# Three more second-layer groups by seven products, in a new static order, with four late stores issued by ScalarE

## The chip, the core and the metric

The kernel runs on one core of one Trainium2 chip. The metric is the device time of one execution in microseconds (us). TensorE is called PE below, VectorE DVE, ScalarE ACT, GpSimd POOL, and SyncE SP; SP issues nearly all DMAs.

## The reference

An attention with random features is followed by a two-layer network with a residual. All is float32; the batch is 8, there are 8 heads, 576 positions per sequence, head width 64, 128 features, model width 512 and hidden width 2048.

```python
def phi(x):
    proj = np.einsum('bhsd,md->bhsm', x, omega)
    h = proj - np.sum(x * x, axis=-1, keepdims=True) / 2.0
    h = h - np.max(h, axis=-1, keepdims=True)
    return np.exp(h) / np.sqrt(m)
q_p, k_p = (phi(q * scale), phi(k * scale))
kv = np.einsum('bhsm,bhsd->bhmd', k_p, v)
num = np.einsum('bhsm,bhmd->bhsd', q_p, kv)
den = np.einsum('bhsm,bhm->bhs', q_p, np.sum(k_p, axis=2))[..., None] + 1e-06
...
x = (num / den).transpose(0, 2, 1, 3).reshape(B, S, H * D)
xn = (x - mu) / np.sqrt(var + 1e-06) * g_ln
out = x + np.maximum(xn @ w_ch1, 0.0) @ w_ch2
```

## The kernel before

The 4608 rows of x are cut into 36 chunks of 128 rows, and four chunks make a tile of 512. Tiles 0 to 2 go through the two layers in the plain way (`mm1`, `mm2`): for each of 16 slabs of 128 hidden columns, a first-layer product, a relu on ACT and DVE, and a second-layer product that adds into four banks. Tiles 3 to 8 go in three pairs (pair 0, 1 and 2, `gen_pair`). A number is kept as two parts, a high and a low one, and a product is three matmuls: high by high, high by low, low by high.

The first layer of a pair takes two slabs of hidden columns at a time (`one_set`), as a 2 by 2 block product that is done with seven products instead of eight (`product`, 6 matmuls of 512 columns each); the sums of inputs and weights that it needs are made beforehand on DVE (`gen_forms` for the inputs, called A11, S1, S2 and so on; `gen_wform` for the weights), and the partial results are combined in the PSUM banks by copies on ACT and additions on DVE (`gen_copy`, `gen_snap`, `gen_x2`, `gen_y2`).

The second layer of a pair is done in four groups of four slabs, after each two sets. In pairs 0 and 1 a group is plain: eight calls of `one_chunk`, each 12 matmuls of 512 columns for one chunk of 128 rows, 96 in all. In pair 2 a group is two calls of `two_chunks`, each seven products of 12 matmuls of 256 columns (`product2`), 168 in all. The hidden values then need sums and high and low parts of their own (`form_a11` to `form_s4`, `finish`), and so do the second-layer weights (`gen_w2form`).

The attention is woven in between: a block of keys (`gen_k`), the sums over keys (`gen_sums`), the queries' features (`gen_q`) and x itself (`gen_x`) are short visits to PE between the large matmuls, each with work on ACT, DVE and, for the queries' maximum, on POOL. A visit of `gen_k`, `gen_sums` or `gen_x` has matmuls of 64 rows or 64 columns.

Nothing is scheduled on the chip: `Plan` runs on the host, keeps a clock for each engine by fixed costs, and writes the instructions of each engine in one order. The dictionary `SLOT` says at which place of PE's stream each visit is to stand (32 units to a tile, so 160 is the start of pair 1), `SHIFT` moves ranks of parts, and `EARLIER`, `WF`, `MARGIN` and others set costs and due times. Each engine then runs its instructions strictly in the order written, and a wait holds up all that stands behind it on that engine.

```python
        wide = p == NPAIR - 1
...
            if p == NPAIR - 1:
                for h in range(2):
                    yield from two_chunks(gr, h)
                continue
```

Of the kernel before, what the change touches and what calls it, by code (L numbers as in the profile page):

```python
# [75 lines left out]
class Plan:  # L76
# [25 lines left out]
    def __init__(self):  # L102
# [12 lines left out]
        self.pair, self.loan, self.at, self.where = (), (), 0, 0  # L115
# [83 lines left out]
    def go_to(self, at, step):  # L199

        self.at, self.step, self.turn = at, step, 0

    def serve(self, lend):
# [11 lines left out]
        sets = (self.pair,) + (lend and len(due) > 1) * (self.loan,)  # L215
# [10 lines left out]
        if lend and len(cols) == len(todo) > 2 and guests:  # L226
# [74 lines left out]
    def run(self):  # L301
        while self.ready or self.stuck():
# [24 lines left out]
            if eng == SP:  # L327
# [6 lines left out]
                part.end = self.dma_at + (FLOWN if part.want[-1] == "flip" else 0.0)  # L334
# [12 lines left out]
def favor_ffn(ctx, tc, kT, kTr, vF, vR, qT, qD, omT, gT, w1, w2, out):  # L347
# [86 lines left out]
    def slots(pair):  # L434
        i = 512 * int(pair[0][1:])
        return all_banks.rearrange("p a b -> p (a b)")[:, i : i + H * SLOT].rearrange("p (a b) -> p a b", b=SLOT)[:, :, 0 : D + 1]

# [9 lines left out]
    n_hid, n_xnT, n_mb, n_st = names("hid", 2), names("xnT", 1), names("mb", 3), (*names("st", 3), "st3")  # L447
# [3 lines left out]
    turn = {k: names(f"turn_{k}", n) for k, n in (("k", 2), ("q", 2), ("blk", 3), ("mx", 2), ("xn", 3), ("w", 3), ("wl", 5))}  # L451
# [10 lines left out]
    plan.pair, plan.loan = b_at, b_h  # L462
# [413 lines left out]
    def gen_x(c, b_turn):  # L876
# [13 lines left out]
        t_x = yield "get", n_x  # L890
# [105 lines left out]
    def gen_flip(t, i, xn, t_n, xn_turn):  # L996
# [7 lines left out]
        if t >= NREG + 2:  # L1004
            p, u = divmod(t - NREG, 2)
            yield wait("stage", p)
            cols = slice(u * T + i * P, u * T + (i + 1) * P)
            words = stages[p][1].bitcast(U16).rearrange("p k (c b) -> p b k c", b=2)
            eng = yield either(1.27, 1.13)
            copy(eng, words[:, :, :, cols], flipped)  # L1010
            free(t_n, xn_turn, t_p)
            done(("xT", t, i))
            return
# [4 lines left out]
        if t >= NREG:  # L1018
            u = t - NREG
            yield dma(P * DM, -0.4)  # L1020
            nc.sync.dma_start(
                xT_away[:, :, u * T + i * P : u * T + (i + 1) * P], f32(whole).rearrange("p (a b) c -> p a (b c)", b=P)
            )
            free(t_p)
            done(("xT", t, i))
            return
# [125 lines left out]
    def store(c, t_x, x, p, last):  # L1152
        yield dma(P * (p.stop - p.start), -1.1)
        nc.sync.dma_start(out[c * P : (c + 1) * P, p], x[:, p])
        if last:
            free(t_x)

    n_form = ("A11", "S3", "S2", "A12", "S1", "A22", "S4")
# [6 lines left out]
    xT_away = dram.tile([P, NK, 2 * T], F32, tag="xT_away", name="xT_away", bufs=1)  # L1165
# [4 lines left out]
    hforms, fs, w2q, users, halves_left = {}, {}, {}, {}, {}  # L1170
# [61 lines left out]
    def gen_more():  # L1232
# [8 lines left out]
        extra[n_st[-1]] = more[:, 1, 0:48]  # L1241
        free(n_x[N_X + 2], n_st[-1])

    def gen_stage(p):

        if p:
            yield wait("used", 1, NF - 1)
            yield wait("formed", p - 1)
            t_s = yield "get", n_xnT
            st = tile_of(t_s, [P, NK, 2 * T])  # L1250
            stages[p] = [t_s], st
            done(("stage", p))
# [10 lines left out]
        for k in range(NK):  # L1263
            plan.add(plan.cur.rank, gen_stage_k(p, k))

    def gen_stage_k(p, k):
        yield dma(P * 2 * T)
        nc.sync.dma_start(stages[p][1][k], xT_away[:, k])
# [9 lines left out]
    def gen_forms(p):  # L1278
        if p:
            for u in range(2):  # L1280
                for i in range(TC):
                    yield wait("xT", NREG + 2 * p + u, i)
        else:
            for k in range(NK):
                yield wait("xk", p, k)
# [3 lines left out]
        def cut(ap):  # L1289
            return [ap] if n_part == 1 else [ap[:, k] for k in range(2)]  # L1290
# [7 lines left out]
        def split(name, src):  # L1298
            tags, hi, lo = yield from room(name)
            for o, a in zip(cut(hi), src):  # L1300
                yield us(ACT, 0.22 + 0.00083 * 2 * T / n_part)
                nc.scalar.copy(out=o, in_=a)
            for o, a, b in zip(cut(lo), src, cut(f32(hi))):
                yield dve2(2 * T / n_part)
# [4 lines left out]
        def summed(out_, a, b, op):  # L1309
            for o, x, y in zip(out_, a, b):  # L1310
                yield dve2(2 * T / n_part)
                nc.vector.tensor_tensor(out=o, in0=x, in1=y, op=op)

        yield from split("A11", a11)
        t_s = yield "get", n_quad
        s1 = cut(tile_of(t_s, [P, 2, T]))
        yield from summed(s1, a21, a22, ALU.add)
        yield from summed(a21, a11, a21, ALU.subtract)
        yield from split("S3", a21)
        yield from summed(a11, s1, a11, ALU.subtract)  # L1320
        yield from split("S2", a11)
        yield from split("A12", a12)
        yield from split("S1", s1)
        free(t_s)
        yield from split("A22", a22)
        yield from summed(a12, a12, a11, ALU.subtract)
        yield from split("S4", a12)
        free(*stages[p][0])
        done(("formed", p))

# [26 lines left out]
    def gen_ring2(p):  # L1357
        if p:
            yield wait("w2all", p - 1)
        for f in range(NF):  # L1360
# [4 lines left out]
    def gen_w2(p, f, t_w):  # L1365
# [6 lines left out]
        users[p, f] = 2 if p == NPAIR - 2 else 1  # L1372
        done(("w2s", p, f))

    def leave(p, f):
        users[p, f] -= 1
        if not users[p, f]:
            free(w2s[p, f][0])

    def gen_w2form(j):  # L1380
        f, g = 2 * j, 2 * j + 1
        for n in (f, g):
            yield wait("w2s", NPAIR - 2, n)
# [572 lines left out]
```

## Time and profile before

| | before |
|---|---|
| median of 3 runs | 930.6 us (930.43 to 930.69) |
| profiled execution, its own time | 930.92 us |
| span of its instructions | 929.2 us |
| PE busy | 921.2 us, 99% of the span |
| DVE busy | 673.6 us, 72% |
| ACT busy | 503.1 us, 54% |
| POOL busy | 121.1 us, 13% |
| DMA queue of SP | 201.34 MB, 65.6% of 16 DMA engines' time |
| granted clock of PE | 1.00 (2.4 GHz) |

The span runs from the first to the last instruction; the time of an execution is 1.7 us more. PE's busy time joins the modelled spans of its matmuls, which overlap, so how closely it is packed is better read from the starts of matmuls that follow each other. Idle time of the other engines costs nothing unless PE waits for them.

### The profile page before, as it was taken

Reading aid. Unit: us, or ns where it says so; the run is one execution under the profiler, and the core shown is the slowest. Engines: PE = TensorE matmul, PEld = TensorE weight load, DVE = VectorE, ACT = ScalarE, POOL = GpSimd, SP = SyncE. Lnnn points to the kernel's source line nnn. Section 1 sums busy time; section 2 is a strip of 40 time slices with the busy share of each in tenths; the row PEclk is TensorE's granted clock in tenths of the full one; section 3 lists DMA queues with packets and bytes.
Section 4 is the critical chain, followed back from the end, with each engine's and each line's share of the span. In section 5 each row is a group of like instructions: output and inputs, shape, how many; then the busy total and the mean of one; then the engine's idle time right before and its main releaser. Section 6 shows DMA issues by size and latency. Waiting matters only on the chain.

```text
span 929.2 us, 17577 instructions
## 1 busy us (share of the span) xinstructions
PE 921.2 (99%) x6871; PEld 766.9 (83%) x6871; DVE 673.6 (72%) x1178; ACT 503.1 (54%) x915; POOL 121.1 (13%) x47
## 2 busy tenths in 40 slices
PE   9999999999999999999999999999999999999998
PEld 6878777888888888888888888888888888988988
DVE  6999988674758877667566547898836596585765
ACT  7878876565753472437756444557412245253452
POOL 5001314130420041001302110304000000000000
PEclk9999999999999999999999999999999999999999
DMA  8676369996446559295956634796946558574562
GB/s 310 218 269 238 142 180 365 371 347 167 126 115 233 183 152 341 94 369 118 288 176 202 187 110 174 240 385 150 314 149 225 204 203 298 166 285 141 177 226 91
DMA packets 142577, 202.71 MB, mean 218 GB/s; under 512 B 44064, under 2 KB 79008, under 8 KB 142496
## 3 DMA queue, kind: packets, MB, share of 16 engines
q1 hardware_dynamic: 142352, 201.34, 65.6%
q8 instruction: 54, 0.88, 0.4%
q10 hardware_dynamic: 144, 0.26, 0.1%
q14 instruction: 27, 0.22, 0.1%
HBM read 140.74 MB, written 52.43 MB: 208 GB/s over the span
## 4 chain that ended last, share of the span: by engine, by line
PE 92%; DVE 6%; issue 1%; DMA 0%; SPq 0%; ACT 0%; DVEq 0%
PE b L1423 8%; PE b L1425 8%; PE b L1424 8%; PE b L1745 6%; PE b L1746 6%; PE b L1747 6%; PE b L1122 5%; PE b L1078 4%; PE b L1124 4%; PE b L1123 4%; PE b L1080 4%; PE b L1079 4%; PE b L674 4%; PE b L718 3%; PE b L899 3%; PE b L1665 3%
## 5 line engine op out<-in xcount | busy, mean ns | idle before, releaser
L845 POOL PARTITION_ALL_REDUCE quad<-quad x35 | 118.2, 3398 | 517.3 <-ACT quad L392 380.8
L1423 PE MATMUL b<-w,w 128*128 128x512 f32 x336 | 131.9, 392 | 0.0
L1425 PE MATMUL b<-w,w 128*128 128x512 f32 x336 | 130.8, 389 | 0.0
L1424 PE MATMUL b<-w,w 128*128 128x512 f32 x336 | 130.8, 389 | 0.0
L1745 PE MATMUL b<-w,w 128*128 128x512 f32 x256 | 101.2, 395 | 0.0
L1746 PE MATMUL b<-w,w 128*128 128x512 f32 x256 | 99.8, 390 | 0.0
L1747 PE MATMUL b<-w,w 128*128 128x512 f32 x256 | 99.7, 389 | 0.0
L683 ACT ACTIVATE kp<-b,mb 128x128 f32<-128x128 f32 x264 | 72.3, 389 | 26.8 <-DVE mb L677 25.9
L1122 PE MATMUL b<-w,hid 128*128 128x512 f32 x192 | 78.1, 407 | 0.0
L1078 PE MATMUL b<-xnT,w 128*128 128x512 f32 (+1 forms) x200 | 78.1, 390 | 0.0
L1080 PE MATMUL b<-xnT,w 128*128 128x512 f32 (+1 forms) x200 | 76.2, 381 | 0.0
L1079 PE MATMUL b<-xnT,w 128*128 128x512 f32 (+1 forms) x200 | 76.2, 381 | 0.0
L1124 PE MATMUL b<-w,hid 128*128 128x512 f32 x192 | 75.2, 392 | 0.8 <-DVE hid L1096 0.8
L1123 PE MATMUL b<-w,hid 128*128 128x512 f32 x192 | 75.0, 390 | 0.0
L1423 PEld LDWEIGHTS b<-w,w 128*128 128x128 f32 x336 | 63.1, 188 | 14.2 <-ACT b L1481 0.9
L1487 ACT COPY hid<-b 128x512 f32<-128x512 f32 x64 | 37.6, 587 | 68.1 <-PE b L1425 38.7
L1425 PEld LDWEIGHTS b<-w,w 128*128 128x128 f32 x336 | 63.1, 188 | 13.3
L1424 PEld LDWEIGHTS b<-w,w 128*128 128x128 f32 x336 | 63.1, 188 | 12.7
L1481 ACT COPY b<-b 128x512 f32<-128x512 f32 x32 | 18.6, 580 | 83.6 <-PE b L1425 67.8
L1494 DVE TENSOR_TENSOR b<-b,hid 128x512 f32<-128x512 f32 x32 | 22.3, 697 | 56.5 <-ACT hid L1487 56.3
L1096 DVE SCALAR_TENSOR_TENSOR hid<-b,hid 128x512 fp32r<-128x512 f32 x48 | 33.0, 688 | 37.9 <-ACT hid L1094 37.5
L1745 PEld LDWEIGHTS b<-w,w 128*128 128x128 f32 x256 | 48.0, 188 | 10.8
(220 smaller groups left out, 2050.8 us busy)
## 6 DMA issues: line engine op xcount, KB each, us to landing
w<-wf SPq DMA_DIRECT2D x168, 256.0 KB, 5.0
w<-w SPq DMA_DIRECT2D x32, 512.0 KB, 6.6
w<-w2a SPq DMA_DIRECT2D x32, 512.0 KB, 5.7
quad<-qD SPq DMA_DIRECT2D x28, 512.0 KB, 5.1
away<-x SPq DMA_DIRECT2D x33, 256.0 KB, 2.8
w2a<-w SPq DMA_DIRECT2D x16, 512.0 KB, 6.2
wf<-wide SPq DMA_DIRECT2D x32, 256.0 KB, 2.8
w2t<-wide SPq DMA_DIRECT2D x32, 256.0 KB, 3.1
```

The costliest lines, as they stand in the source:

```text
L845: nc.gpsimd.partition_all_reduce(mx.rearrange("p a b -> p (a b)"), qc.rearrange("p a b -> p (a b)"), P, bass_isa.ReduceOp.max)
L1078: nc.tensor.matmul(ph[:, ts], w[:, 0, cs], xnT[:, 0, k, ts], start=k + i0 == 0, stop=False)
L1079: nc.tensor.matmul(ph[:, ts], w[:, 1, cs], xnT[:, 0, k, ts], start=False, stop=False)
L1080: nc.tensor.matmul(ph[:, ts], w[:, 0, cs], xnT[:, 1, k, ts], start=False, stop=k == NK - 1 and i1 == TC)
L1122: nc.tensor.matmul(accs[i][:, c], hl[:, 0, cs], w[:, 0, c], start=(f == 0), stop=False)
L1124: nc.tensor.matmul(accs[i][:, c], hl[:, 1, cs], w[:, 0, c], start=False, stop=f == NF - 1 and c == parts[-1])
L1423: nc.tensor.matmul(o, w[:, 0, cs], hi[:, k], start=first and k == 0, stop=False, skip_group_check=True)
L1424: nc.tensor.matmul(o, w[:, 1, cs], hi[:, k], start=False, stop=False, skip_group_check=True)
L1425: nc.tensor.matmul(o, w[:, 0, cs], lo[:, k], start=False, stop=k == 1, skip_group_check=True)
L1745: nc.tensor.matmul(acc[:, o], hl[:, 0, cs], w[:, 0, o], start=n == 0 and o is parts[0], stop=False)
L1746: nc.tensor.matmul(acc[:, o], hl[:, 0, cs], w[:, 1, o], start=False, stop=False)
L1747: nc.tensor.matmul(acc[:, o], hl[:, 1, cs], w[:, 0, o], start=False, stop=n == 3 and o is parts[-1])
```

## The change

One constant, `G1 = 1`, says that in pair 1 only the first group stays plain; groups 1, 2 and 3 take the two calls of `two_chunks` that pair 2 had. So 288 matmuls of 512 columns go and 504 of 256 columns come. What goes with it:

- The hidden forms are made for these groups too: on DVE and ACT `form_a11` and the like run 14 times each instead of 8.
- The weights' forms (`gen_w2form`) are made before pair 1's second group instead of during pairs 1 and 2, from high and low parts that are loaded for it (32 loads of 256 KB more).
- The inputs of pairs 1 and 2 go through DRAM as pair 0's did (16 stores of 256 KB and 8 loads of 512 KB more) instead of being written into place. Their room lends eight more buffers for x.
- All attention visits must be over before pair 1's second group: the last `gen_x` has slot 168 instead of 179.
- `Plan` may serve visits in a third pair of banks, so that more of them can follow each other directly.
- In the last group of pairs 1 and 2, two of the stores are issued from ACT's queue.
- `SLOT`, `SHIFT`, `EARLIER` and the cost constants are all new, so nearly every engine's order differs.

```diff
+G1 = 1
+ORDERED = 7
+STAGE, FORM_AT, FORM_LAST = ((2, 3, 4, 5), (4, 5, 6, 6)), 7, 22
+W2GO = 19
-W2F = -30
+W2F = (240, 25)
-MARGIN = {ACT: 0.2, DVE: 0.15}
-FLOWN, EDGE = 1.2, (0.1, 0.1)
+MARGIN = {ACT: 0.2, DVE: 0.1}
+FLOWN, EDGE = 1.2, (1.1, 0.1)
-WF = (35, 15.0)
+WF = (46, 19.0)
...
+    def strassen2(p, gr):
+
+        return p == NPAIR - 1 or (p == NPAIR - 2 and gr >= G1)
...
-            if p == NPAIR - 1:
+            if strassen2(p, gr):
                 for h in range(2):
-                    yield from two_chunks(gr, h)
+                    yield from two_chunks(p, gr, h)
                 continue
...
-        sets = (self.pair,) + (lend and len(due) > 1) * (self.loan,)
+        sets = (self.pair,) + self.where * (self.third,) + (lend and (len(due) > 1 or self.where > 0)) * (self.loan,)
...
+        for i in range(2):
+            plan.add(plan.cur.rank, gen_w2in(2 * j + i, r[i], low[i]))
...
+    def gen_w2in(f, r, low):
+        yield dma(2 * P * DM, 0.5)
+        nc.sync.dma_start(r, w2_away[f][:, 0])
+        nc.sync.dma_start(low, w2_away[f][:, 1])
+        done(("w2in", f))
...
-    def store(c, t_x, x, p, last):
-        yield dma(P * (p.stop - p.start), -1.1)
-        nc.sync.dma_start(out[c * P : (c + 1) * P, p], x[:, p])
+    def store(c, t_x, x, p, last, by_act=False):
+        if by_act:
+            yield us(ACT, 0.45)
+        else:
+            yield dma(P * (p.stop - p.start), -1.1)
+        (nc.scalar if by_act else nc.sync).dma_start(out[c * P : (c + 1) * P, p], x[:, p])
...
-                plan.add(MOST_URGENT, store(c, t_x, x, cols, not halves_left[c]))
+                plan.add(MOST_URGENT, store(c, t_x, x, cols, not halves_left[c], h == half == i == 1))
```

**First place: PE, the end of the second set of pair 1's group 1 and what follows.** Before (`b` is a PSUM bank; the lines 1745 to 1747 are `one_chunk`'s three matmuls):

```order
L1423 MATMUL b_74<-w1_100_6139,w2_10_3495 128x512
L1424 MATMUL b_74<-w1_100_6139,w2_10_3495 128x512
L1425 MATMUL b_74<-w2_90_6140,w2_10_3495 128x512
L1745 MATMUL b_74<-w2_100_6727,w1_130_6813 128x512
L1746 MATMUL b_74<-w2_100_6727,w1_130_6813 128x512
L1747 MATMUL b_74<-w2_100_6727,w1_130_6813 128x512
```

Of the change, at the same place (lines 1719 to 1721 are `product2`'s):

```order
L1463 MATMUL b_74<-w1_100_6513,w2_10_3489 128x512
L1464 MATMUL b_74<-w1_100_6513,w2_10_3489 128x512
L1465 MATMUL b_74<-w2_90_6514,w2_10_3489 128x512
L1719 MATMUL b_74<-w2_100_7014,kp0_7079 128x256
L1720 MATMUL b_74<-w2_100_7014,kp0_7079 128x256
L1721 MATMUL b_74<-w2_100_7014,kp0_7079 128x256
```

The 96 rows of 512 columns that stood here have become 168 of 256.

**Second place: DVE in tile 0, where the first-layer weights of slab 9 get their low half** (line 604 is `gen_w`'s last subtraction, 1096 and 1089 the relu's low half, 580, 566 and 588 steps of other weights). Before, as DVE's rows 135 to 139:

```order
L566 SCALAR_TENSOR_TENSOR w2_90_1062<-w2_90_1062,wide4_1136 128x512
L394 CAST w1_90_1176<-wide6_1081 128x512
L400 TENSOR_SCALAR w2_90_1062<-w2_90_1062 128x512
L1096 SCALAR_TENSOR_TENSOR hid1_1159<-b_74,hid1_1159 128x512
L604 TENSOR_TENSOR w1_90_1176<-wide6_1081,w1_90_1176 128x512
```

Of the change, DVE's rows 150 to 155:

```order
L588 TENSOR_TENSOR wide2_1210<-wide2_1210,g_sb_83 128x512
L1089 SCALAR_TENSOR_TENSOR hid0_1277<-b_74,hid0_1277 128x512
L580 SCALAR_TENSOR_TENSOR wide1_1265<-w1_110_1157 128x512
L566 SCALAR_TENSOR_TENSOR w1_130_1165<-w1_130_1165,wide4_1281 128x512
L949 BN_AGGR st0_440<-st0_440 128x2
L604 TENSOR_TENSOR w1_90_1302<-wide2_1210,w1_90_1302 128x512
```

PE's first matmul of that slab stands at nearly the same place in both (row 385 before, 386 of the change), and DVE comes to its weights 16 instructions later, behind the relu of slab 8 instead of beside that of slab 7. Up to DVE's row 60 (the relu of slab 0) and PE's row 214 the two orders of these engines are the same, buffer numbers and one low half of weights (DVE's row 59) aside.

**Third place: the last stores.** Before, SP's last rows:

```order
L1154 DMA out<-x5_7845 128x256
L1154 DMA out<-x2_7885 128x256 x2
L1154 DMA out<-w2_140_4349 128x256 x2
L1154 DMA out<-w2_150_4372 128x256
L1154 DMA out<-x5_7845 128x256
```

Of the change, SP's last rows are the first four here, and ACT's last two rows (after its last copy, line 1534) are the fifth and sixth:

```order
L1150 DMA out<-w2_150_4353 128x256
L1150 DMA out<-x0_8413 128x256 x2
L1150 DMA out<-x2_8429 128x256
L1150 DMA out<-w2_140_4327 128x256
L1150 DMA out<-x2_8429 128x256
L1150 DMA out<-w2_150_4353 128x256
```

The store of the last result, `w2_150`, now stands on a queue that has issued one other store since its last copy.

## Rows read from the trace of the kernel before

**Rows 1.** The page, busy time, share of the span and instructions of each engine

```profile
PE 921.2 (99%) x6871; PEld 766.9 (83%) x6871; DVE 673.6 (72%) x1178; ACT 503.1 (54%) x915; POOL 121.1 (13%) x47
```

**Rows 2.** Timeline, pair 1, group 1: start, length, engine, line; first and next after

```profile
664.16 0.39 PE L1745 MATMUL b<-w,w 128*128 128x512 f32 x1
...
685.92 0.39 PE L1423 MATMUL b<-w,w 128*128 128x512 f32 x1
```

**Rows 3.** Timeline, PE's waits for DVE: idle before and releaser in brackets

```profile
39.48 0.50 PE L1124 MATMUL b<-w,hid 128*128 128x512 f32 x1 [0.29 <-DVE hid L1096]
...
128.15 0.49 PE L1124 MATMUL b<-w,hid 128*128 128x512 f32 x1 [0.54 <-DVE hid L1096]
...
151.84 0.50 PE L833 MATMUL b<-quad,om_hi 128*128 128x512 f32 x1 [0.46 <-DVE kv L746]
...
484.95 0.47 PE L833 MATMUL b<-quad,om_hi 128*128 128x512 f32 x1 [0.16 <-DVE x L910]
```

**Rows 4.** Timeline, pair 2, groups 0 and 2: first matmul, next after

```profile
786.68 0.28 PE L1665 MATMUL b<-w,kp 128*128 128x256 f32 x1
...
806.99 0.40 PE L1423 MATMUL b<-w,w 128*128 128x512 f32 x1
...
826.18 0.28 PE L1665 MATMUL b<-w,w 128*128 128x256 f32 x1
...
846.22 0.40 PE L1423 MATMUL b<-w,w 128*128 128x512 f32 x1
```

**Rows 5.** Timeline, PE around one visit alone and around two together

```profile
304.08 0.39 PE L1124 MATMUL b<-w,hid 128*128 128x512 f32 x1
304.40 2.09 PE L899 MATMUL b<-kv,quad 128*64 128x65 f32 x64
...
306.75 0.40 PE L1123 MATMUL b<-w,hid 128*128 128x512 f32 x1
...
337.09 0.39 PE L1124 MATMUL b<-w,hid 128*128 128x512 f32 x1
337.41 1.15 PE L899 MATMUL b<-kv,quad 128*64 128x65 f32 x32
...
338.83 0.40 PE L1123 MATMUL b<-w,hid 128*128 128x512 f32 x1
```

**Rows 6.** Timeline, the last operations

```profile
924.57 0.87 DVE L1719 SCALAR_TENSOR_TENSOR w<-b,st,w 128x256 f32<-128x256 f32 x2
924.79 1.41 SPq L1154 DMA_DIRECT2D out<-w  x3
925.36 0.48 DVE L1719 SCALAR_TENSOR_TENSOR x<-b,st,x 128x256 f32<-128x256 f32 x1
926.29 0.41 SPq L1154 DMA_DIRECT2D out<-x  x1
```

**Rows 7.** Windows in tile 0 and pair 2: stretch, length, busy time of each engine, clock, DMA

```profile
39.50:99.50 60.00, 60.00 (x422) 47.11 (x424) 59.97 (x109) 49.73 (x108) 5.37 (x2) 1.00 0.70 252
...
768.00:925.00 157.00, 156.83 (x1007) 142.58 (x1005) 105.89 (x192) 68.36 (x120) 0.00 (x0) 1.00 0.59 199
```

**Rows 8.** The chain in order of time, 108 to 111 us: start, length, what

```profile
109.71 0.60 DVE w L604
110.31 1.14 DVE quad L850
```

**Rows 9.** Timeline, POOL's reductions and DVE beside them

```profile
97.37 8.98 POOL L845 PARTITION_ALL_REDUCE quad<-quad  x2 [22.77 <-ACT quad L392]
...
102.58 2.98 DVE L580 SCALAR_TENSOR_TENSOR wide<-w 128x512 uint32<-128x512 uint32 x2
...
124.71 2.13 DVE L394 CAST w<-wide 128x512 fp32r<-128x512 f32 x1
```

**Rows 10.** Windows with full DMA engines, pair 1 and tile 1; columns as in rows 7

```profile
605.00:627.00 22.00, 22.00 (x152) 17.99 (x151) 21.15 (x49) 12.62 (x19) 0.00 (x0) 1.00 1.07 389
...
139.40:232.00 92.60, 92.14 (x853) 74.21 (x852) 64.29 (x116) 57.17 (x109) 20.30 (x6) 1.00 0.97 313
```

More of the change, by code (lines that the diff above doesn't have):

```diff
@@ L114, in __init__ @@
         self.mlp = None
-        self.pair, self.loan, self.at, self.where = (), (), 0, 0
+        self.pair, self.loan, self.third, self.at, self.where, self.zone = (), (), (), 0, 0, 0
         self.shared = {}
@@ L197, in lodge, with go_to @@
         self.shared.update(dict.fromkeys(four, 0.0))
-    def go_to(self, at, step):
-        self.at, self.step, self.turn = at, step, 0
+    def go_to(self, at, zone, where, step):
+        self.at, self.zone, self.where, self.step, self.turn = at, zone, where, step, 0
     def serve(self, lend):
@@ L225, in serve @@
         guests = [p for p in cols if p.want[3]]
-        if lend and len(cols) == len(todo) > 2 and guests:
+        if lend and not self.where and len(cols) == len(todo) > 2 and guests:
             todo.remove(guests[0])
@@ L333, in run @@
                 self.landed.append(self.dma_at)
-                part.end = self.dma_at + (FLOWN if part.want[-1] == "flip" else 0.0)
+                part.end = self.dma_at + (FLOWN if part.want[-1] == "flip" else 0.0) + LAND * late
             else:
@@ L889, in gen_x @@
         total = st[:, 44 + i : 45 + i]
-        t_x = yield "get", n_x
+        if t >= ORDERED:
+            yield wait("place", c - 1)
+        t_x = yield "get", n_x + n_room
+        done(("place", c))
         t_d = yield "get", n_dn
@@ L1359, in gen_ring2 @@
             yield wait("w2all", p - 1)
-        for f in range(NF):
+        for f in range(NF if p < NPAIR - 2 else 4 * G1):
             t_w = yield "get", n_ring2
@@ L1544, in form_a11, with form_a22 @@
         free(b_a)
-        done(("f", j, "A11"))
-        yield from finish(j, "A11")
-    def form_a22(j, s):
-        a22 = yield from whole(j, "A22")
+        done(("f", p, j, "A11"))
+        yield from finish(p, j, "A11")
+    def form_a22(p, j, s):
+        a22 = yield from whole(p, j, "A22")
         eng = yield either(0.5, 0.34)
@@ L1555, in form_a22, with form_a21 @@
         free(s)
-        done(("f", j, "A22"))
-        yield from finish(j, "A22")
-    def form_a21(j, b_c):
+        done(("f", p, j, "A22"))
+        yield from finish(p, j, "A22")
+    def form_a21(p, j, b_c):
         rank = plan.cur.rank
-        a21 = yield from whole(j, "A21")
+        a21 = yield from whole(p, j, "A21")
         yield act(T)
@@ L1599, in form_a12, with form_s4 @@
             free(b_b)
-    def form_s4(j, b_b, left_b):
-        yield wait("f", j, "S2")
-        yield wait("a12", j)
-        s4 = yield from whole(j, "S4")
+    def form_s4(p, j, b_b, left_b):
+        yield wait("f", p, j, "S2")
+        yield wait("a12", p, j)
+        s4 = yield from whole(p, j, "S4")
         yield dve(T)
         nc.vector.scalar_tensor_tensor(
-            out=s4, in0=bank(b_b), scalar=0.0, in1=fs[j, "S2"][1], op0=ALU.max, op1=ALU.subtract
+            out=s4, in0=bank(b_b), scalar=0.0, in1=fs[p, j, "S2"][1], op0=ALU.max, op1=ALU.subtract
         )
@@ L1659, in product2 @@
             w = w2q[t_w]
-            for i in range(2):
-                o = bank(t_b)[:, i * HALF : (i + 1) * HALF]
-                cs = slice((2 * h + i) * P, (2 * h + i + 1) * P)
-                yield us(PE, 0.36)
-                fresh, last = first and i == s == 0, s == 1
-                nc.tensor.matmul(o, hl[:, 0, cs], w[:, 0], start=fresh, stop=False, skip_group_check=True)
-                nc.tensor.matmul(o, hl[:, 0, cs], w[:, 1], start=False, stop=False, skip_group_check=True)
-                nc.tensor.matmul(o, hl[:, 1, cs], w[:, 0], start=False, stop=last, skip_group_check=True)
@@ L1668, in product2 @@
-            if h:
-                free(tag, t_w)
-    def two_chunks(gr, h):
-        ta, j = NREG + 2 * (NPAIR - 1), NF + 2 * gr + h
-        b_a, b_d, b_b, b_c = (banks[0], banks[1], banks[6], banks[7]) if h == 0 else (banks[2], banks[3], banks[5], banks[4])
-        sk, p = snaps[h], NPAIR - 1
+            o = bank(t_b)[:, i * HALF : (i + 1) * HALF]
+            cs = slice((2 * h + i) * P, (2 * h + i + 1) * P)
+            yield us(PE, 0.36)
+            fresh, last = first and i == s == 0, s == 1
@@ new lines, in product2, with two_chunks @@
+            nc.tensor.matmul(o, hl[:, 0, cs], w[:, 0], start=fresh, stop=False, skip_group_check=True)
+            nc.tensor.matmul(o, hl[:, 0, cs], w[:, 1], start=False, stop=False, skip_group_check=True)
+            nc.tensor.matmul(o, hl[:, 1, cs], w[:, 0], start=False, stop=last, skip_group_check=True)
+            if h and i:
+                free(tag, t_w)
+    def two_chunks(p, gr, h):
+        ta, j = NREG + 2 * p, NF + 2 * gr + h
+        b_a, b_d = b_acc[2:4] if h else b_at
+        b_b, b_c = turned()
+        sk = snaps[h]
```

318 lines of the change are left out of this document (176 added, 142 removed).

## The prediction

> **What bounds the kernel now.** I read the page's busy shares first: PE is busy 99% of the span, and no other engine over 73% [rows 1]. Since a matmul's span is modelled and overlaps the next one, I then read the starts of matmuls in a plain group of pair 1: its 96 matmuls of 512 columns take from 664.16 to 685.92 us, 21.76 us [rows 2], or 0.227 us each without a gap. From 39.5 us to the end the whole stream looks like that, but for the short attention visits and four places where PE waits for DVE [rows 3]. An idle time there begins at the modelled end of a matmul, about 0.16 us after the place where the next start would have been; with that added the four waits are 0.46, 0.70, 0.62 and 0.32 us, together 2.1 us. So the time is PE's work, plus the first 39 us, in which the two orders agree, plus these waits, plus the tail after the last matmul. Anything that takes matmuls away shortens the kernel, unless DVE, ACT or the DMA queue comes too late for the shorter stream.
>
> **What the change costs, part by part.**
>
> The matmuls. Three groups of 96 matmuls of 512 columns go. What comes in their place exists in pair 2: 168 matmuls of 256 columns take 20.04 us in its group 2 (826.18 to 846.22) and 20.31 us in its group 0 (786.68 to 806.99, with a small wait in it) [rows 4]. A group so gains 1.45 to 1.72 us, three gain 4.4 to 5.2; I take 4.9. The gain is small because a narrow matmul costs 20.04 / 168 = 0.119 us, more than half of 0.227. The Trainium skill, "TensorE: Matmul & The Clock Gate", section "Back-to-back issue gap", gives a gap of columns / 2.4 GHz and some 2.5 ns at full clock. By that the gain would be 288 x 0.2158 - 504 x 0.1092 = 7.1 us. The trace does not agree with the page, both sizes run about 11 ns longer here, and the trace decides.
>
> The visits. Their number and kinds stay, but more of them follow each other directly. A visit alone costs, from the start of the last large matmul to the start of the second one behind it, 338.83 - 337.09 = 1.74 us, less two steps of 0.227: 1.29 us. Two together cost 306.75 - 304.08 - 0.45 = 2.22 us [rows 5]. So a visit is 0.93 us of work and a turn of PE between large and small matmuls 0.36 us. Counting in the two orders the places where PE turns to visits with 64 rows or columns after the first large matmul, I find 64 before and 59 now: 5 x 0.36 = 1.8 us less. Bounds: 0, if the pieces that now meet in new mixes pay a change of kind of their own, and 2.2.
>
> The tail. The last DVE operation ends at 925.36 + 0.48 = 925.84 us, but its store is issued at 926.29, because SP's queue is busy with three earlier stores until 926.20 [rows 6]. On ACT's queue, idle by then, it can start at about 925.95: 0.35 us less; bounds 0 and 0.45.
>
> Tile 0. From 39.5 to 99.5 us DVE is busy 59.97 of 60.00 us [rows 7]: here weights are split, and DVE is as much the bound as PE. A step of 512 elements costs DVE 0.60 us when it runs back to back, one of 1024 elements 1.14 [rows 8]. Both orders agree up to the relu of slab 0, which ends at 39.4 us. In the new order the low half of slab 9's first-layer weights comes 95 DVE instructions later: 79 of 0.60, 5 of 1.14 and 11 short ones, 54.2 us, so at 93.6 us. PE gets to that slab after 180 large matmuls and 11 visits in 8 turns: 40.9 + 10.2 + 2.9 = 54.0 us from 39.0, so at 93.0: a wait of about 0.6 us. Before, those weights stood 16 instructions earlier and were no limit. The relu of slab 11 is DVE's 145th instruction from there: 81.4 us, at 120.8 us at the earliest. PE reaches it after 264 matmuls and 19 visits in 13 turns, 82.3 us, at 121.3, and some 0.7 us later if its steps drift as they did before. But DVE is held up now and then: two steps that should take 1.2 us took 2.98, and one that should take some 0.35 took 2.13, both while POOL reduced; with a wait for PE the relu of slab 12 before was so about 4.1 us later than its count [rows 9], which made the wait at 128.15. Held up as much, DVE would give PE 2.9 us of waits in the new order; not held up at all, 0.6. Before it was 0.70. I take 1.7, so 1.0 us more; bounds -0.1 and +2.8.
>
> The other two waits, at 151.84 and 484.95 us, 0.94 us together, belong to DVE results that now stand elsewhere. I take half of it as gone: -0.5; bounds -0.9 and +1.
>
> The step from pair 1 to pair 2. Its input forms (seven splits and four sums of 1024 elements, 12.5 us of DVE) are made during the last two calls of `two_chunks`, 20.1 us, beside two bank additions of 0.60, two more into SBUF and sixteen half-chunk updates of 0.40 (two start within 925.36 - 924.57 = 0.79) [rows 6]: 8.8 us. That is 21.3 us of DVE in 20.1 of PE, and the form that the third product needs comes, counted through, some 0.4 us late. I take 0.4; bounds 0 and 2.
>
> Transfers. Between the weight loads of pair 0's group 1 and those of its group 3, SP's order now has 121 DMAs with 37.3 MB, before 78 with 24.4 MB: x goes through DRAM, the weights' forms are made here, and queries come sooner. PE takes 102 us for these two groups (360 large matmuls, 20 visits), so this asks for 366 GB/s. The trace has full engines twice: 389 GB/s at a share of 1.07, and 313 GB/s at 0.97 in a stretch with many transposes and strided stores [rows 10]; PE waited in neither for a load. At 389 the stretch needs 96 us and hides. At 313 it needs 119, 17 us too long, of which the ring of eight loaded weight pieces (one per product of 6 x 0.227 = 1.36 us) hides 10.9. I take a loss of 1.0 us, nearer to the first since the weight ring's plain loads are the larger part; bounds 0 and 6.3.
>
> DVE's and ACT's other new work (six forms of pair 1, 36 more halves by `finish`) lies beside sets of PE: in pair 2, where all groups are of this kind, DVE is busy 105.89 of 157 us and ACT 68.36 [rows 7], and PE does not wait there.
>
> Sum: -4.9 - 1.8 - 0.35 + 1.0 - 0.5 + 0.4 + 1.0 = -5.15 us. The profiled execution, 930.9 us with 929.2 of span, is 0.3 us above the median; from the median of 930.6 that makes **925.5 us**.
>
> **The rivals.**
>
> DVE gives the gain back in tile 0. If POOL's reductions fall on DVE's steps as often as three times before slab 11 and twice more before slab 14, PE waits 2.9 + 1.8 instead of 1.7 us: 928.5 us. For it speaks that DVE has no idle time from 39.5 to 99.5 us; against it that PE's wait is counted once, whichever of the two slabs it stands before.
>
> Slower: the DMA engines fall behind in pair 0's groups 1 and 2. The mechanism is a load of first-layer weights that stands in SP's order behind transposes and stores, and a product that waits for it. At 300 GB/s the 37.3 MB take 124 us, 22 more than PE, of which 11 are hidden: 11.4 us in place of the 1.0, 935.9 us. It decides at about 313 GB/s, where 5.3 us more than forecast bring the time back to what it was; below that the kernel is slower. For it: 1.5 times the bytes of before in that stretch, and 313 seen. Against: 389 seen as well, and all four waits of PE are for DVE, none for a load [rows 3].
>
> More gain than forecast: no wait for DVE is left, turns at 2.2 and groups at 5.2 us: -5.2 - 2.2 - 0.4 - 2.1 + 0 = -9.9 at the very most; with half of the waits left 922.3 us.
>
> The change saves matmuls but nothing comes out: waits of 0.5 us scattered over ten new places. Nothing in the trace before speaks for a place; the stream after 155 us has one wait. 930 us.
>
> **How the numbers follow.** Forecast 0.60 (its own range 923.5 to 927.3), DVE in tile 0 0.15, slower by DMA 0.08, more gain 0.08, scattered waits 0.09. The range leaves out the upper part of the slower case and of the scattered waits and most of the extra gain: 923.0 to 929.5 us. A change of 0.2%, 1.9 us, is about what a measurement tells from none here: below 928.7 is faster. Faster: 0.60 + 0.08 + 0.75 of 0.15 and a small part of the scattered waits = 0.81; same: 0.10; slower: 0.09.
>
> **What would show it.** Right: groups 1 to 3 of pair 1 with second layers of 20.0 to 20.3 us; PE busy near 915 us; a wait of PE before slab 9 and one before slab 11 of tile 0, together 0.6 to 2.9 us; the last DMA issue on ACT's queue within 0.15 us of DVE's last end; full DMA engines around 450 to 550 us and no PE wait there over 1 us. Wrong: releasers of PE that are DMAs of weight pieces in pair 0; DVE waits over 3 us in tile 0; more than a few tenths at the step from pair 1 to pair 2; or new waits of PE for ACT, which the sum holds at nothing because ACT is busy only 54% of the span [rows 1].

## The result, and the profile after

The changed kernel takes 936.0 us (median of 4 runs, 935.43 to 937.97) against 930.62 us (930.43 to 930.69, 4 runs): 1.0056 times as long, interval 1.0044 to 1.0069. It was forecast at 925.5 us with a range of 923.0 to 929.5, so it moved the other way. The profiled execution is the longest of the four, 937.97 us with a span of 936.2.

The page of the changed kernel: busy time by engine, the DMA engines' share in 40 slices of the span, and the queue of SP.

```profile
PE 919.6 (98%) x7087; PEld 774.5 (83%) x7087; DVE 706.5 (75%) x1278; ACT 522.9 (56%) x959; POOL 118.3 (13%) x47
...
DMA  8666469993457487599996979697838478483562
...
q1 hardware_dynamic: 163760, 222.32, 71.3%
```

PE's share is 98% where it was 99% [rows 1]. That line alone would hardly tell that the span grew by 7.0 us: this is less than one per cent. The row of DMA shares shows where to look: from the 18th slice (398 us) to the 26th (608 us) its digits are 9 9 9 9 6 9 7 9 6.

First, the part that came out as counted. The second-layer groups of pair 1, first matmul of the group and the next one after it, timeline of the changed kernel:

```profile
676.16 0.28 PE L1719 MATMUL b<-w,kp 128*128 128x256 f32 x1
...
696.21 0.40 PE L1463 MATMUL b<-w,w 128*128 128x512 f32 x1
...
754.62 0.28 PE L1719 MATMUL b<-w,w 128*128 128x256 f32 x1
...
774.95 0.40 PE L1463 MATMUL b<-w,w 128*128 128x512 f32 x1
```

Groups 1 and 3 take 20.05 and 20.33 us (group 2 is as long as group 1) where a plain one took 21.76 [rows 2]: 4.9 us less for the three.

Then PE's waits, over the whole span after the start (line, what released it: idle time in all, how often, the longest):

```profile
PE b L1463 <- ACT hid L1534: 2.4, 1, 2.4
PE b L902 <- ACT quad L392: 2.0, 1, 2.0
PE b L1463 <- ACT b L1528: 2.0, 2, 1.6
PE b L674 <- DVE x L913: 1.0, 2, 0.6
PE b L674 <- ACT kp L683: 0.9, 1, 0.9
PE b L1115 <- ACT hid L1087: 0.7, 1, 0.7
...
```

With five groups more, of 1.9 us in six waits, these 14 waits are 10.9 us idle, and with the 0.16 us that each costs beyond its idle time 13.1 us; before, it was 2.1 us in four waits, all for DVE [rows 3]. Of the 10.9 us, 8.5 are now for ACT, an engine that is busy 56% of the span. Behind the wait at 470 us the granted clock fell to the lower level for some 3 us (shown below), which is 1.6 us more. So the span's 7.0 us are: -4.9 for the matmuls, -0.8 for the tail (from the start of PE's last matmul to the end 3.9 us instead of 4.7), +11.0 for waits, +1.6 for the clock, and 0.1 that is left for everything else, the turns of PE among them. This run is 2.0 us above the median of its kernel, so some of its waits are longer than usual.

Why does PE wait for an engine that is half idle? The chain in the changed kernel's trace around 520 us, in order of time (start, length, what):

```profile
513.87 6.10 DMA w2t<-wide
...
520.05 0.06 ACT wide L1003
...
521.00 1.33 ACT wide L392
522.33 0.49 ACT b L1528
...
522.87 0.50 PE b L1463
```

A store of a second-layer weight form (`w2t`, 256 KB) took 6.1 us from its issue to its landing. ACT's copy at line 1003 writes into the buffer that this store empties (`wide`, a ring of eight that weights, x and keys share), so it can't start before 520.05. ACT runs in order, and behind that copy and another one (line 392) stands line 1528, the copy that frees a bank for PE's next product: PE starts at 522.87 instead of some 521.1. No wait of PE in this stretch is for what the copy at line 1003 itself makes. The place near 615 us reads the same way:

```profile
610.33 6.28 DMA w2t<-wide
...
616.69 0.19 ACT wide L986
...
617.32 0.57 ACT hid L1534
...
617.94 0.50 PE b L1463
```

And near 470 us, from the timeline, with the store of the transposed x in the place of `w2t`:

```profile
468.89 1.05 ACT L1003 COPY wide<-wide 128x1024 uint16<-128x1024 uint16 x1 [1.19 <-DMA xTa<-wide]
...
470.33 0.59 ACT L1528 COPY b<-b 128x512 f32<-128x512 f32 x1
...
471.80 1.00 ACT L392 COPY quad<-b 128x1024 f32<-128x1024 f32 x1
...
472.86 1.16 PE L902 MATMUL b<-kv,quad 128*64 128x65 f32 x32 [2.03 <-ACT quad L392]
```

Here ACT stands 1.19 us for the store and PE 2.03 us for ACT, so the store explains at most 1.2 us of PE's wait; for the rest ACT is busy with its own work, from 468.89 us up to line 392.

How full the DMA engines are there, in windows (columns as in [rows 7]: the last but one is the share of the DMA engines, the last GB/s). Of the changed kernel:

```profile
390.00:530.00 140.00, 134.90 (x1211) 109.97 (x1208) 113.87 (x201) 90.81 (x161) 36.74 (x11) 0.99 0.95 292
530.00:620.00 90.00, 87.58 (x504) 71.71 (x503) 64.64 (x112) 35.03 (x58) 6.55 (x2) 1.00 0.83 296
```

And of the kernel before, for the same times:

```profile
390.00:530.00 140.00, 139.84 (x1128) 115.41 (x1126) 87.36 (x152) 80.11 (x147) 21.39 (x7) 1.00 0.75 232
530.00:620.00 90.00, 90.00 (x609) 74.26 (x608) 66.21 (x101) 41.63 (x67) 11.49 (x4) 1.00 0.59 204
```

From 0.75 to 0.95, and from 0.59 to 0.83. PE lost 5.1 and 2.4 us of busy time in these two windows, and nearly nothing before the change.

### The profile page after: what moved, and what is told of

The parts are those of the page before. It is cut to its first block, busy times and chain, and to the rows that moved or that the text cites. A ratio compares the mean times of both kernels' runs of the same rounds, so it can differ in the third digit from the quotient of the medians.

```text
span 936.2 us, 18332 instructions
## 1 busy us (share of the span) xinstructions
PE 919.6 (98%) x7087; PEld 774.5 (83%) x7087; DVE 706.5 (75%) x1278; ACT 522.9 (56%) x959; POOL 118.3 (13%) x47
## 3 DMA queue, kind: packets, MB, share of 16 engines
q1 hardware_dynamic: 163760, 222.32, 71.3%
## 4 chain that ended last, share of the span: by engine, by line
PE 83%; DVE 10%; DMA 3%; ACT 2%; issue 1%; SPq 1%; DVEq 0%; ACTq 0%
PE b L1463 8%; PE b L1465 7%; PE b L1464 7%; PE b L1071 5%; PE b L1115 4%; PE b L1721 4%; PE b L1719 4%; PE b L1720 4%; PE b L1117 4%; PE b L1072 4%; PE b L1073 4%; PE b L1116 4%; PE b L718 4%; PE b L674 4%; PE b L1803 3%; PE b L1805 3%
## 5 line engine op out<-in xcount | busy, mean ns | idle before, releaser
L845 POOL PARTITION_ALL_REDUCE quad<-quad x35 | 115.4, 3321 | 499.8 <-ACT quad L392 242.3
L1463 PE MATMUL b<-w,w 128*128 128x512 f32 x336 | 133.8, 398 | 4.4 <-ACT hid L1534 2.4
L1465 PE MATMUL b<-w,w 128*128 128x512 f32 x336 | 131.5, 391 | 0.3 <-DVE w L1309 0.3
L1464 PE MATMUL b<-w,w 128*128 128x512 f32 x336 | 131.5, 391 | 0.0
L1534 ACT COPY hid<-b 128x512 f32<-128x512 f32 x76 | 44.8, 590 | 84.8 <-PE b L1721 45.5
L683 ACT ACTIVATE kp<-b,mb 128x128 f32<-128x128 f32 x264 | 74.3, 394 | 21.6 <-DVE mb L677 21.3
L1463 PEld LDWEIGHTS b<-w,w 128*128 128x128 f32 x336 | 63.4, 189 | 20.6 <-ACT b L1528 4.5
L1465 PEld LDWEIGHTS b<-w,w 128*128 128x128 f32 x336 | 63.4, 189 | 14.4 <-DVE w L1309 0.7
L1541 DVE TENSOR_TENSOR b<-b,hid 128x512 f32<-128x512 f32 x38 | 26.4, 695 | 63.9 <-ACT hid L1534 63.9
L1464 PEld LDWEIGHTS b<-w,w 128*128 128x128 f32 x336 | 63.5, 189 | 12.3
L1803 PE MATMUL b<-w,w 128*128 128x512 f32 x160 | 63.3, 396 | 0.0
L1804 PE MATMUL b<-w,w 128*128 128x512 f32 x160 | 62.4, 390 | 0.0
L1805 PE MATMUL b<-w,w 128*128 128x512 f32 x160 | 62.3, 389 | 0.0
L1528 ACT COPY b<-b 128x512 f32<-128x512 f32 x38 | 22.0, 578 | 68.9 <-PE b L1465 43.0
L677 DVE TENSOR_REDUCE mb<-b 128x8 f32<-128x1024 f32 x36 | 43.4, 1216 | 13.8 <-PE b L674 13.0
```

What stands on the lines that cost most here:

```text
L845: nc.gpsimd.partition_all_reduce(mx.rearrange("p a b -> p (a b)"), qc.rearrange("p a b -> p (a b)"), P, bass_isa.ReduceOp.max)
L1463: nc.tensor.matmul(o, w[:, 0, cs], hi[:, k], start=first and k == 0, stop=False, skip_group_check=True)
L1464: nc.tensor.matmul(o, w[:, 1, cs], hi[:, k], start=False, stop=False, skip_group_check=True)
L1465: nc.tensor.matmul(o, w[:, 0, cs], lo[:, k], start=False, stop=k == 1, skip_group_check=True)
L1803: nc.tensor.matmul(acc[:, o], hl[:, 0, cs], w[:, 0, o], start=n == 0 and o is parts[0], stop=False)
L1805: nc.tensor.matmul(acc[:, o], hl[:, 1, cs], w[:, 0, o], start=False, stop=n == 3 and o is parts[-1])
```

## The experiments

Theory A was: the transfers between 390 and 620 us come late, ACT and DVE stand behind them in their order, and PE behind these. Its main rival, B: the new order itself is too tight for ACT and DVE, and the late transfers are only a companion.

**Fewer bytes, the same order.** Three kernels keep every engine's order and thin transfers of two kinds. What stands for the first (with the later loads of the forms turned to other weights of the same size):

```diff
-            nc.vector.tensor_tensor(out=r[i], in0=r[i], in1=low[i], op=ALU.add)
+            nc.vector.tensor_tensor(out=r[i], in0=r[i], in1=r[i], op=ALU.add)
...
-        nc.sync.dma_start(low, w2_away[f][:, 1])
...
-        nc.sync.dma_start(w2t_away[j][:, 2 * i : 2 * i + 2, k], f32(src))
+        nc.sync.dma_start(w2t_away[j][:, 2 * i : 2 * i + 2, k, : HALF // 4], f32(src)[:, :, : HALF // 4])
```

> The order of every engine stays that of the changed kernel (936.0 us). What is left out: the low halves that the second-layer weights' sums are made from are not loaded (16 loads of 256 KB), the 32 stores of those sums write a quarter of their columns, and the later loads of the sums read other weights of the same size. So 10.5 MB less pass in the stretch from 388 to 640 us, and DVE and ACT do the same work. Theory A (transfers are late, ACT and DVE stand behind them in their order, and PE behind these): the PE waits near 517 us and 615 us (1.8 and 2.6 us), where ACT waits for the stores of these sums, go, and some of those near 400 and 470 us: 930 to 932 us. Rival B (the new order itself makes ACT and DVE too late, the transfers only follow): 935 to 937 us.

It takes 930.05 us, 0.9993 times the kernel before (0.9984 to 1.0001). The second thins the stores of the transposed x:

```diff
-                xT_away[u // 2][:, :, ...], f32(whole).rearrange("p (a b) c -> p a (b c)", b=P)
+                xT_away[u // 2][:, :1, ...], f32(whole).rearrange("p (a b) c -> p a (b c)", b=P)[:, :1]
...
-        nc.sync.dma_start(place, xT_away[p][:, k])
+        nc.sync.dma_start(place, xT_away[p][:, 0])
```

> The order stays that of the changed kernel. What is left out: the 24 stores of the transposed x write a quarter (64 KB instead of 256 KB each), and the loads read that quarter four times over, so that they are as large as before; 4.7 MB less. Theory A: the wait at 470 us (2.0 us and some 1.5 us of lower clock behind it), in which ACT stands behind such a store, goes, and some of those at 460 and 517 us: 931 to 934 us. Rival B: 935 to 937 us.

931.97 us, 1.0014 times (1.0004 to 1.0025). And both together:

> Both edits of the two kernels before it: 15 MB less between 388 and 660 us, the same order. Theory A: nearly all PE waits between 390 and 620 us go, 11 us: 925 to 928 us. Rival B: 934 to 937 us. If the two single edits give back as much together as this one, the stores delay different things; if this one gives more than their sum, the load of the DMA engines as a whole counts.

929.52 us, 0.9982 times (0.9973 to 0.9990): 6.5 us less than the changed kernel's median, and 5.9 and 4.0 us for the single edits. (By the two ratios to the kernel before, whose runs beside this one took 931.09 us, the 6.5 are 6.9.) So theory A holds for some 6.5 us, and B falls. But the 925 to 928 us that were expected did not come: 11 us were counted in the longest of the runs, not every wait in this stretch is the transfers' doing, and this kernel's trace has two waits of PE for second-layer weights, 0.25 and 0.35 us idle at 753 us, that the changed kernel's has not. What is left of PE's waits from 390 to 620 us with both edits:

```profile
PE b L718 <- ACT quad L392: 0.5, 1, 0.5
PE b L833 <- DVE quad L828: 0.2, 1, 0.2
```

Against 7.4 us in the changed kernel. The two single edits give back more than the pair does together: which fits two ways of clearing one queue, though no run tests that.

**The four stores on ACT's queue, undone.**

```diff
-                plan.add(MOST_URGENT, store(c, t_x, x, cols, not halves_left[c], h == half == i == 1))
+                plan.add(MOST_URGENT, store(c, t_x, x, cols, not halves_left[c]))
```

> The four stores go back to the sync engine's queue, everything else as in the changed kernel. The tail of the changed kernel is 0.7 us shorter than before (last matmul to end 3.9 instead of 4.6 us); if the stores on ACT's queue are the reason, 0.4 to 0.7 us more than the changed kernel: 936.4 to 936.7 us, and the last store is issued 0.3 to 0.5 us after the last DVE operation. If the queue is not the reason, 936.0 us.

935.22 us, 1.0045 times (1.0029 to 1.0061). This is below the range that was expected, and the interval overlaps that of the changed kernel, so by time this part can't be told from nothing: the runs of this kernel spread over 5 us, those of the thin one over 1.5. The rows tell it. The end in the changed kernel (DVE's last operation, and the issue of its store):

```profile
933.09 0.48 DVE L1776 SCALAR_TENSOR_TENSOR w<-b,w 128x256 f32<-128x256 f32 x1
...
933.59 0.34 ACTq L1150 DMA_DIRECT2D out<-w  x1
```

With the stores back on SP's queue:

```profile
928.34 0.48 DVE L1776 SCALAR_TENSOR_TENSOR w<-b,w 128x256 f32<-128x256 f32 x1
928.78 0.90 SPq L1150 DMA_DIRECT2D out<-w  x2
```

On ACT's queue the store is issued 0.02 us after its data. On SP's it is the second of two that take 0.90 us, so it begins at about 929.23, 0.41 us after its data. The term holds: some 0.4 us. This profile, of a run of 933.67 us, also shows how much the waits change from run to run in nearly the same order: at the three places where the changed kernel's longest run has PE idle for 2.0, 1.6 and 2.4 us, it has 0.4, 0.8 and 1.6.

**A transpose by DMA made a plain copy.** Is it those two kinds of stores, because ACT waits for their buffers, or the load of the DMA engines as a whole?

```diff
-        nc.sync.dma_start_transpose(out=flipped..., in_=halves...)
+        if t >= NREG:
+            nc.sync.dma_start(flipped..., halves...)
+        else:
+            nc.sync.dma_start_transpose(out=flipped..., in_=halves...)
```

> The order stays that of the changed kernel (936.0 us), and all its bytes are moved. What is left out: from tile 3 on, the 24 transposes that a DMA makes of x (256 KB each) are plain copies from and to the same places. Theory A (the DMA engines as a whole are over-full from 390 to 530 us, and it does not matter which transfer is made lighter): if a transpose takes the engines clearly longer than a plain 256 KB transfer (0.7 us at 360 GB/s), the PE waits behind ACT near 400, 470 and 517 us go, as in the kernel with less of both kinds: 929 to 931 us, and the queue's share of the engines' time falls by 2 to 4 points from 71%. Rival A2 (only the stores of the second-layer weights' sums and of the transposed x matter, since it is their buffers that ACT waits for): 934 us or more.

931.12 us, 1.0000 times (0.9991 to 1.0009), so by the times rival A2 falls: 4.9 us come back with every byte still moved. The rows bear the expectation out in part. Of PE's waits that were to go, the one near 470 us is gone, but 0.3 us are left at 406 and 1.1 at 518 us, and 1.7 near 613, the latter two behind stores of `w2t` as before (lines 1466, 1531 and 1537 here are 1463, 1528 and 1534 of the changed kernel):

```profile
PE b L1466 <- ACT hid L1537: 1.7, 1, 1.7
PE b L1466 <- ACT b L1531: 1.5, 2, 1.1
```

The profiled run is the longest of its eleven, 933.31 us. The first window of this kernel:

```profile
390.00:530.00 140.00, 137.72 (x1239) 112.69 (x1236) 115.43 (x203) 92.40 (x164) 36.72 (x11) 1.00 0.87 310
```

The share falls from 0.95 to 0.87 where most of the transposes are, and the rate rises. Over the span the queue's share is 68.6% of 931.5 us instead of 71.3% of 936.2: 28.5 us of all 16 engines less for 24 transposes, 1.2 us each. A plain 256 KB transfer takes 0.7 us at the rate of the full windows in [rows 10] (389 GB/s at a share of 1.07), so by this estimate a transpose takes about 1.9 us, 2.6 times as long. The Trainium skill, "Advanced Engine Details and Errata", section "X-Bar Transpose (TRN2)", says that transposing DMAs are as fast as regular ones on TRN2; this kernel's trace does not agree. The planner charges a transpose 0.9 us, half of what it takes.

**What is left before 390 us.** The waits near 168 and 272 to 279 us are in the thin kernel too. The timeline of the changed kernel at the second of them:

```profile
271.74 0.69 DVE L947 BATCH_NORM_STATS2 st<-x 128x6 f32<-128x512 f32 x1
...
272.57 0.69 DVE L913 SCALAR_TENSOR_TENSOR x<-b,dn 128x512 f32<-128x512 f32 x1
...
273.32 1.16 PE L674 MATMUL b<-om,wide 64*128 64x128 f32 x16 [0.61 <-DVE x L913]
```

Two x visits (each a matmul group and DVE's work on its result) follow each other directly here, 12 large matmuls stand behind them, and then a visit of keys that needs a bank which DVE still reads. In the thin kernel DVE's statistics were made short:

```diff
-        nc.vector.bn_stats(bn, x)
+        nc.vector.bn_stats(bn, x[:, :D])
```

> The kernel with both thin transfers (929.5 us), and DVE's row statistics of x read 64 columns instead of 512 (36 instructions, some 0.5 us less each; the statistics are then those of 64 columns). Theory C (the PE waits that are left at 168 and from 272 to 279 us, 2.9 us together, come from DVE's work behind two x visits that now stand close before the next visit: results of x, statistics, then the maximum of the next keys): they shrink by 1.5 us or more, 927.0 to 928.3 us. Rival D (they hang on ACT or on the banks alone): no change, 929.0 to 930.0 us.

928.90 us, 0.9973 times (0.9962 to 0.9985); against 0.9982 of the kernel that it was made from, the intervals overlap. Its waits up to 390 us:

```profile
PE b L674 <- ACT kp L683: 0.9, 1, 0.9
PE b L1115 <- ACT hid L1087: 0.7, 1, 0.7
PE b L1117 <- DVE hid L1089: 0.6, 2, 0.3
PE b L674 <- DVE x L913: 0.4, 1, 0.4
```

Of the two waits for `x` the one at 273 us (0.6) is gone and the one at 168 is still there, and so are the two that follow at 278 us for ACT and DVE. Theory C holds for one wait of four, and the forecast of 1.5 us fails.

**The same work in another order.** If full DMA engines cost time only where ACT or DVE stands behind a transfer with PE's work behind it, another order of the same bytes must do without the loss. The planner was given the price of a transpose that the copies had shown, and its tables were searched anew by its own clock:

```diff
-        yield "run", {SP: 0.9}, "flip"
+        yield "run", {SP: 1.88}, "flip"
...
-W2F = (240, 25)
+W2F = (250, 40)
-WF = (46, 19.0)
+WF = (82, 23.5)
```

and nearly all entries of `SHIFT` (583 of them instead of 231) and 72 of the 115 of `SLOT`.

> All the work and all the bytes of the changed kernel, nothing left out. The one cost that is changed is what the host's planner charges for a transposing DMA: 1.88 instead of 0.9 units of the DMA engines' time, since the kernel with plain copies showed 1.2 us more for each transpose than for a plain copy (0.7 us). With that cost the ranks and visit times of the two tables were searched anew, which puts stores, forms and visits elsewhere. Theory A (the waits came from transfers that the order did not allow for): PE waits behind ACT's waits for stores are gone, all waits of PE together below 5 us, and 924 to 928 us, so faster than before (930.6 us). Rival E (orders for so full a DMA queue miss by some 6 us whatever they charge, since landing times vary): 930 to 935 us.

928.08 us, 0.9970 times (0.9960 to 0.9981): faster than both kernels, and PE has no wait at all from 390 to 620 us. So rival E falls, and the range of theory A is missed by 0.1 us. But is it the price of the transpose, or only the search? The control keeps 0.9 and was searched as well:

> The control of the kernel searched anew: the same search of the two tables, about as long, but a transpose is charged 0.9 as in the changed kernel. The planner's own clock ends 2.3 us earlier than that of the kernel searched with 1.88 (922.0 against 924.3 us). Theory A (the wrong charge for a transpose lets the order run into waits): PE waits behind ACT and stores stand between 390 and 620 us again, 3 us or more in all, and 929 to 934 us. Rival F (the search alone was what helped): 925 to 927 us, 2 us less than with the charge of 1.88.

> The kernel searched anew with a charge of 1.88 once more, beside its control on the same chip. 927.5 to 928.7 us, as it was.

The control takes 926.64 us, 0.9950 times (0.9938 to 0.9963), the other one on the same chip 928.47 us, 0.9973 times (0.9964 to 0.9982). Rival F's range came, and theory A's 929 to 934 us did not: the price of the transpose was not what the order lacked. The windows of the control:

```profile
390.00:530.00 140.00, 139.63 (x1186) 113.52 (x1188) 115.24 (x203) 96.20 (x169) 37.00 (x11) 1.00 0.99 312
530.00:620.00 90.00, 89.70 (x513) 73.64 (x510) 73.97 (x127) 35.80 (x58) 7.04 (x2) 1.00 0.85 298
```

The DMA engines are even fuller than in the changed kernel, 0.99 and 0.85, and PE loses next to nothing. The same holds for the 102 us that the prediction counted for groups 1 and 2 of pair 0, first in the changed kernel, then in the control:

```profile
446.00:548.00 102.00, 97.57 (x755) 79.35 (x752) 74.70 (x128) 64.35 (x111) 27.10 (x8) 0.98 0.97 297
```

```profile
446.00:548.00 102.00, 101.64 (x769) 82.82 (x768) 78.66 (x134) 65.14 (x111) 27.36 (x8) 1.00 0.98 307
```

Nor do the stores of `w2t` land sooner in the control. From 385 to 625 us the median from issue to landing is 5.5 us there, 5.2 in the changed kernel, and 5.7 for the eight such stores of the kernel before. So what differs should be what ACT has to write into their buffers, and when; this is argued from these rows, and no run tests it alone. ACT's waits for transfers from 385 to 620 us, first in the changed kernel, then in the control:

```profile
ACT quad L826 <- DMA quad<-qD: 8.1, 6, 1.9
ACT wide L1003 <- DMA w2t<-wide: 6.8, 2, 3.7
ACT wide L986 <- DMA w2t<-wide: 6.3, 2, 3.5
ACT wide L1003 <- DMA xTa<-wide: 1.2, 1, 1.2
```

```profile
ACT quad L826 <- DMA quad<-qD: 14.7, 5, 8.1
...
ACT wide L986 <- DMA w2t<-wide: 1.1, 1, 1.1
...
ACT wide L1003 <- DMA w2t<-wide: 0.6, 1, 0.6
```

The waits for `w2t` stores fell from 13.1 to 1.7 us. Those for queries grew to 14.7, one of them of 8.1 us, and PE does not feel it: a wait of ACT costs only what stands behind it and is due. The last run tests that:

> The control of the search (926.6 us, a transpose charged 0.9) with the two thin edits: of the second-layer weights' low halves none is loaded, the stores of their sums and of the transposed x write a quarter, 15 MB less between 388 and 660 us; these parts of the computation are left out, the order stays that of the control. In the order of the changed kernel the same edits gave back 6.5 us. Theory A, as it stands now (a full DMA queue costs only where ACT or DVE stands behind a transfer with work for PE behind it, and this order has hardly such a place): at most 1.0 us less, 925.6 to 926.7 us. Rival G (less traffic makes every order faster by about as much, whatever stands where): 920 to 923 us.

925.72 us, 0.9943 times (0.9930 to 0.9957): the two edits that gave 6.5 us in the order of the changed kernel give 0.9 us here, which the two intervals don't tell from nothing, and rival G falls.

## Why the prediction was wrong, step by step

- The matmuls (-4.9): right, 4.9 us. The narrow step of 0.119 us of pair 2 held in pair 1. The 7.1 us that the prediction set beside it are no test of the Trainium skill: the section that it names gives that formula for an isolated matmul, and says that a stream with weight loads goes otherwise.
- The turns of PE (-1.8): too large. By the sum above, 0.2 us of gain is left for them, if the start is counted, which was 0.27 us longer (PE resumes at 39.75 instead of 39.48 us). Added up from the starts of PE's matmuls, with the waits taken out, the places with such visits take 110.1 us before and 109.5 us now, 0.6 us less for five turns fewer. So the price of 0.36 us, read from one pair of visits, does not hold for these; which visits take longer now wasn't tried.
- The tail (-0.35): right in place and size, 0.4 us of earlier issue; the rest of the 0.8 us in the profiled run is the last transfer itself, which varies from run to run.
- Tile 0 (+1.0): wrong place. Slabs 9 and 11 show no wait. The wait that came, 0.9 us at 61 us, is for ACT, whose exponentials of the keys (line 683) hold a bank. The prediction had looked for waits on DVE only, and held new waits for ACT at nothing. With what a wait costs beyond its idle time it is 1.0 us; the one of 0.7 us at 128.15 us is gone, so +0.3.
- The other two waits (-0.5): they went, but others came at 168 (0.4 us idle), 272 to 279 (0.6, 0.7 and 0.3) and 460 us (0.5): 3.3 us with what each costs beyond its idle time, so +2.4 instead of -0.5. This was the rival of scattered waits, and the prediction gave it 0.09 because the stream before had only one such place after 155 us. A new order has places of its own.
- The step from pair 1 to pair 2 (+0.4): right. Group 3 takes 20.33 us, and PE waits 0.3 us idle for the third product's form (line 1309).
- Transfers (+1.0): **the step that failed**. It measured 6.5 us by the thin kernel, and some 9 in the profiled run (PE's waits at 399, 406, 473, 523 and 618 us and the lower clock). The stretch was right for two of the three long waits (473 and 523 us, but not 618), and so was that it asks for more than the engines give: 366 GB/s were asked for, and 297 came from 446 to 548 us, at a share of 0.97. The fault was in how a late transfer reaches PE. The prediction counted what the ring of eight loaded weight pieces hides, as if only loads of first-layer weights could stop PE. No PE wait is for such a load, and one, of 0.3 us at 399 us, is for a load at all (keys). What was late before the three long waits were stores, whose buffers ACT needs again (DVE stands for loads in this stretch, for no store; the 0.4 us at 406 follow a load of queries that ACT waited for), and in an in-order engine the whole rest stands behind, so that PE came to wait for ACT, which the sum held at nothing: a store of 6.1 us kept ACT standing for 3.0 us near 517 us, and PE for 1.6 us.
- The slower rival gave 935.9 us, and 936.0 came; but its mechanism, a product that waits for its weights, isn't what happened, so it was near for a wrong reason. What it had right is that the DMA queue of pair 0 decides the sign, and the rate of some 300 GB/s. But the rate does not decide at 313 GB/s, as it held: the control moves 307 in the same stretch and is faster than the kernel before.
- The rival of more gain: by its own terms, 930.6 - 9.9 and half of the 2.1 us of waits, it gives 921.8 us and not 922.3. Nothing hangs on it.

With most of these waits taken out by order alone, the control comes near what the matmuls and the tail give: 930.6 - 4.9 - 0.4 is 925.3 us, and 0.9950 times 930.6 is 926.0. That this is also near the forecast's 925.5 is in part luck, since the forecast's other terms, several of them wrong, add up to +0.1.

What stays open: which of the many moved rows in the control's order matter, and why it is 0.2% faster than the order searched with the truer price of a transpose. Both orders came out of a search with luck in it, and one of each says little about the price. In the second profile of the latter order PE waits 0.8 us idle for loads of second-layer forms from 750 to 753 us, in the first one and in the control it does not. Nor was the order of the kernel before searched anew, so how far the control's gain over it is the change's, and how far the search's, is not shown.

## What to carry to other kernels

Before a change adds transfers to a stretch whose DMA engines are three quarters busy, list not the loads that the bottleneck reads, but the stores whose buffers an in-order engine writes next, and what stands behind that instruction on that engine: a half-idle engine stops the busiest one that way. Make the test with thinner transfers and the same order; it separates load from order in one run. And when an order is at fault, the count of saved work is not lost: here the same bytes in another order gave it back, at the same load of the DMA engines.

## What the runs showed of the hardware that was not expected

- A transposing DMA of 256 KB within SBUF took the 16 engines about 1.9 us, a plain one 0.7 (the estimate above, from 24 of them replaced).
- After PE had waited 0.55 us at 460.7 and 2.03 us at 470.8 us, the granted clock of the profiled run fell for 3 us. A window of it, at half of the full clock, so at 1.2 GHz, and two of the matmuls' starts, 0.42 us apart instead of 0.227:

```profile
474.00:477.00 3.00, 3.00 (x9) 2.42 (x8) 1.60 (x6) 0.09 (x1) 2.19 (x1) 0.50 1.08 393
```

```profile
475.82 0.63 PE L1464 MATMUL b<-w,w 128*128 128x512 f32 x1
476.24 0.63 PE L1465 MATMUL b<-w,w 128*128 128x512 f32 x1
```

  The wait of 2.4 us at 615 us in the same run was followed by matmuls at full speed.
- The kernels in which PE waits for transfers spread: 932.8 to 937.9 us for six runs of the one with the stores back on SP's queue, against 928.6 to 930.1 for eleven of the thin one. The clock has a part in it: of the twelve runs of the kernel with thin stores of x alone, the four of 934.2 us and more have a mean granted clock of 0.998, the other eight, up to 932.3 us, 0.999 or 1.000.
